# A gated mix of softmax attention and a gated linear unit on Trainium2: row maxima closed per 512 queries and 16 steps ahead, block products added one period later, token sums loaded in quarters, 16 zero products at the start

## The chip, the cores and the metric

The kernel runs on one core of one Trainium2 chip. The metric is the device time of one execution in microseconds, less being better. Before the change three runs took 1696.09, 1696.15 and 1697.68 us; their median is 1696.15 us.

## What is computed

```python
x = A_x                                              # (1, 2048, 512), fp32
g = sigmoid((x * gate_w).sum(-1, keepdims=True))
qkv = x @ wqkv                                       # 32 heads of 16
p = softmax(q @ k.T * 16 ** -0.5)                    # per head, 2048 x 2048
a = (p @ v) @ wo
h = sigmoid(x @ w_gate) * (x @ w_up)                 # 1792 wide
b = h @ w_down
return g * a + (1 - g) * b
```

All of it is fp32. The kernel splits each operand of a large product into a rounded part (h) and its remainder (l) and adds three products: h with h, h with l, l with h.

## The kernel before

**Stages.** The work has four stages, one after the other on TensorE.

1. *Start.* WARM products of zeros (L82) run while the first inputs load; then come the q and k projections of the first 8 heads (L134) and the values of two token tiles.
2. *Head.* The values of the other 14 token tiles are made two tiles at a time. Each pair of tiles takes two groups of 12 pairs of 64-row products (L147), one group for each half of the rows (LOW, UP). Into these groups calls of `first_max` are put. One call makes two products of scores with 48 rows each (L277), one for each head of the pair or for two tiles of the second head, and VectorE takes the maximum of each over 512 keys (L279, `stat`).
3. *Periods.* 256 periods follow. Two heads make a pair of heads, there are 16 pairs, and each pair takes 16 periods. A period makes eight tiles of scores, transposed, with 64 rows, of which two hold the negative row maxima (L670); ScalarE takes their exponentials (L672); 32 narrow products multiply them with the values (L687, `values`). It also makes eight score products and their maxima (L277, L279) for periods still to come, so that a maximum is ready when the exponent needs it. The gaps of TensorE are filled with the rest of the dense work, piece by piece (`filling`): first 24 projections of two periods each (`Sum`, L147), then 196 block products of one period each (`Side`, L167). These block products form the gate and up products by a scheme with seven instead of eight block products, on sums of token blocks (`xm`) and sums of weight blocks (`mh`, `ml`).
4. *Final.* The down projection, and the heads' outputs (L880).

**What sets the order.** Each engine runs its instructions in the order in which the program writes them. Within a period the order on TensorE is written out as words in STEADY: m0 and m1 are a score product with its maximum (`mx`), t0 and t1 a transposed score tile with its exponential (`st_part`), d0 and d1 a half row of the dense work, `turn` a token on GpSimd. The word `work` and a call at the end of each period pop entries from the list `later`: GpSimd operations that belong to the dense work (splits of weights, sums of blocks, sums of tokens). The last TAIL periods have the order LAST, which has no m words. The bank of PSUM that a product takes follows from a fixed recurrence (`given`, REUSE).

**The maxima.** `sm_step` numbers 512 steps. A step is one tile of 128 queries against 1024 keys for both heads of a pair: two calls. In the head of the program the first FIRST steps of pair 0 are made for both heads, those to UPPER for the second head only; from then on `mx(0)` and `mx(1)` go on from there, four products each a period. So the maxima lead the scores by FIRST steps, two steps a period, and the last FIRST/2 periods have no maxima left to make; these are the TAIL periods. When all maxima of one head over 1024 queries are there (32 of them, `full`), `turn_max` (L288 to L301) ends them: VectorE takes the maximum over the four key blocks (L291) and transposes it (L293), GpSimd splits it into two parts (L98, L99), and SyncE stores it (L296, `m_d`) and loads it back as two rows of `qs` (L300). `turn_max` runs after the end of a period.

**Dense helpers.** `mixing` makes sums of token blocks: it loads pieces of x, adds them on GpSimd and stores them in `xm_d`; `mixed` (L350 to L353) loads such a sum of 2 MB as one DMA. `combine` adds block products: its `arrive` puts additions on GpSimd (L399) as soon as the eviction of the product has been written (L494, ScalarE). `split_later` (L121, L124) splits weights on GpSimd, a cast to the rounded part and a subtraction.

Of the kernel before, what the change touches and what calls it, by code (L numbers as in the profile page):

```python
# [35 lines left out]
FIRST = 20  # L36
WARM = 20
# [9 lines left out]
def gated_mix(ctx, tc, x, xc, wqk, wv, wo, w_gu, w_down, gate_w, out):  # L47
# [28 lines left out]
    m_d = dram.tile([NPAIR, 2, 2, P, 2, 32], F32, name="m_d")  # L76
# [187 lines left out]
    def sm_step(j):  # L264
# [5 lines left out]
        def one(b, i):  # L270
            half = (p, qt // 8, b)
            if half not in stat:
                stat[half] = keep.tile([P, 8, 4], F32, name=f"stat{p}_{qt // 8}_{b}", tag="stat", bufs=4)
                count[half] = 0
            r, g = 64 * b, 2 * kh + i
            t = bankm()
            pe.matmul(t, qs[r:r + KM, qt * P:(qt + 1) * P], ks[r:r + KM, g * 512:(g + 1) * 512],  # L277
                      start=True, stop=True)
            dve.tensor_reduce(stat[half][:, qt % 8, g:g + 1], t, axis=AX.X, op=ALU.max)  # L279
            count[half] += 1  # L280
            if count[half] == 32:
                full.append(half)
# [4 lines left out]
    def turn_max():  # L287
        half = full.pop(0)  # L288
        p, i, b = half
        m = square()  # L290
        dve.tensor_reduce(m[:, :8], stat.pop(half), axis=AX.X, op=ALU.max)  # L291
# [6 lines left out]
        for a in range(2):  # L298
            r = 64 * b + 3 * DH + a
            sp.dma_start(QS[p % 2][r:r + 1, i * 1024:(i + 1) * 1024].bitcast(F32).rearrange(  # L300
                "o (t g j) -> o t g j", g=4, j=32), rows[a, :8].unsqueeze(0))  # L301
# [7 lines left out]
    def mixing(pair):  # L309

        def piece(j, b):
# [9 lines left out]
            def add(rows, op):  # L321
                pool.tensor_tensor(f[rows, 0, :], f[rows, 0, :], f[rows, 1, :], op)

            def low():
                pool.tensor_tensor(e[:, 0, :], f[:, 0, :], f[:, 1, :], ALU.subtract)
                sp.dma_start(xm_d[pair, j, :, :, b, :], f)
            ops = []
            signs = [MIX[j][1 - g][1] for g in (LOW, UP)]
            if signs[0] == signs[1]:
                rows = [slice(0, P)]  # L330
            else:
                rows = SIDES
            for r, sign in zip(rows, signs):
                if sign:
                    ops.append(lambda r=r, op=ALU.add if sign == "+" else ALU.subtract: add(r, op))
            ops.append(lambda: pool.tensor_copy(e[:, 1, :], f[:, 0, :]))
            ops.append(low)
            return ops

        ops = []  # L340
        for j in range(4):
            for b in range(4):
                nxt = piece(j, b)
                later.extend(ops)
                ops = nxt
                yield
        later.extend(ops)
        yield

    def mixed(pair, j):  # L350
        t = xp.tile([P, 2, KT, 512], F32R, name=f"xm{pair}_{j}", tag="xt", bufs=4)
        sp.dma_start(t.bitcast(F32), xm_d[pair, j])
        return t  # L353

# [69 lines left out]
    def filling():  # L424
# [41 lines left out]
        t = 0  # L466
        for cp in range(2):
            for fp in range(NF // 2):
                for a in range(2):
# [3 lines left out]
                    for q, (j, g) in enumerate(order):  # L473
# [7 lines left out]
                        arrive(m, e)  # L481
# [5 lines left out]
                        if cp == 0 and fp == NF // 2 - 1 and a == 1 and q in (2, 4, 6):  # L487
                            late_t[q // 2 - 1] = mixed(1, q // 2 - 1)
                if cp == 0 and fp == NF // 2 - 1:
                    late_t[3] = mixed(1, 3)  # L490
                    T = late_t
        wd.extend(split_weights(raw_weights(w_down[f * P:(f + 1) * P, :], [P, D], f"wd{f}")) for f in range(2))
# [439 lines left out]
```

## Time and profile before

| what | time in us |
|---|---|
| median of three runs | 1696.15 |
| the profiled execution | 1695.68 |
| its span, first to last instruction | 1693.4 |
| start: zero products, then real ones from 8.33 | 0.92 to 35.65 |
| head: values of 14 tiles with 44 calls of `first_max` | 35.65 to 91.02 |
| passage from the head to the first `values` | 91.02 to 97.95 |
| periods: 256 `values`, the last one starts at | 1491.68 |
| final stage to the end of the span | 1493.6 to 1693.4 |

The profile is that of one execution. Its own time is 0.47 us below the median of the runs, and 2.3 us of it lie outside the span. Engines are named PE (TensorE), DVE (VectorE), ACT (ScalarE), POOL (GpSimd) and SP (SyncE, which only issues DMAs here). Over the whole span PE has work in hand for 99%, DVE for 84%, ACT for 79%, POOL for 59%. Products of PE overlap, so a busy PE can still be one that waits for a bank of PSUM; the start times of its products tell more than the busy share.

### The profile page before, as it was taken

To read this page: it belongs to the slowest core of one execution; us is meant where nothing else is said; L and a number is where in the kernel's file an instruction comes from. 1 tells how busy PE (TensorE), PEld (TensorE's weight loads), DVE (VectorE), ACT (ScalarE), POOL (GpSimd) and SP (SyncE) were. 2 spreads that over 40 slices of the span, in tenths; PEclk is the share of its full clock that TensorE was granted. 3 is DMA by queue.
4 is the path that set the end of the run, shared out by engine and by line. 5 is a ranking of instruction groups with operands and counts; after the bars stand their busy time and mean duration, and the time that the engine had idled before them with its cause. 6 is when DMAs were issued, how large, how long until landed. Compare 5 with 4: busy or idle time off the path is not lost.

```text
span 1693.4 us, 42705 instructions
## 1 busy us (share of the span) xinstructions
PE 1683.5 (99%) x16556; PEld 1151.9 (68%) x16556; DVE 1427.4 (84%) x2321; ACT 1338.7 (79%) x2677; POOL 999.7 (59%) x1065
## 2 busy tenths in 40 slices
PE   9999999999999999999999999999999999999998
PEld 8766666666666666666666666666666666478887
DVE  5988898898898898898898899888889889757543
ACT  4178888888888888888888899999999989974321
POOL 1036665357878787766666667777776665442110
PEclk9999999999999999999999999999999999999999
DMA  9514776363545454442447242524242522367752
GB/s 259 111 51 156 177 246 192 109 186 103 131 136 129 142 142 132 118 125 78 98 136 239 71 122 83 113 83 110 87 112 84 116 89 97 97 220 240 243 192 67
DMA packets 132170, 229.55 MB, mean 136 GB/s; under 512 B 30784, under 2 KB 47424, under 8 KB 127936
## 3 DMA queue, kind: packets, MB, share of 16 engines
q1 hardware_dynamic: 131680, 226.30, 46.8%
q8 instruction: 130, 2.13, 0.5%
q14 instruction: 72, 0.59, 0.1%
q10 hardware_dynamic: 288, 0.52, 0.1%
HBM read 148.90 MB, written 77.86 MB: 134 GB/s over the span
## 4 chain that ended last, share of the span: by engine, by line
PE 96%; DVE 3%; ACT 1%; issue 0%; POOL 0%; DVEq 0%; POOLq 0%; ACTq 0%
PE dn L167 23%; PE sm L687 22%; PE sm L277 9%; PE st L277 8%; PE st L687 7%; PE sm L880 7%; PE dn L147 6%; PE sm L670 4%; PE st L134 4%; PE st L670 3%; DVE stat L279 3%; PE dn L880 2%; ACT p L672 1%; PE st L147 0%; PE st L82 0%
## 5 line engine op out<-in xcount | busy, mean ns | idle before, releaser
L279 DVE TENSOR_REDUCE stat<-sm 128x1 f32<-128x512 f32 x1129 | 726.6, 682 | 68.7 <-PE sm L277 26.7
L672 ACT ACTIVATE p<-sm 128x512 f32<-128x512 f32 x1211 | 675.6, 638 | 2.2 <-PE sm L670 0.3
L279 DVE TENSOR_REDUCE stat<-st 128x1 f32<-128x512 f32 x919 | 600.3, 683 | 71.2 <-PE st L670 28.3
L672 ACT ACTIVATE p<-st 128x512 f32<-128x512 f32 x837 | 494.2, 643 | 10.5 <-PE st L670 9.4
L167 PE MATMUL dn<-xm,mh 64*128 64x512 f32 x1568 | 485.3, 389 | 0.0
L670 PE MATMUL sm<-qs,ks 64*128 64x512 f32 x1211 | 436.3, 404 | 0.3 <-ACT p L672 0.2
L277 PE MATMUL sm<-ks,qs 48*128 48x512 f32 x1129 | 412.4, 421 | 1.2 <-DVE stat L279 0.7
L687 PE MATMUL sm<-p,v 128*17 128x256 f32 x6176 | 370.9, 380 | 0.1
L277 PE MATMUL st<-ks,qs 48*128 48x512 f32 x919 | 352.1, 426 | 0.7 <-ACT p L672 0.7
L670 PE MATMUL st<-qs,ks 64*128 64x512 f32 x837 | 318.9, 409 | 1.5 <-ACT v L539 1.4
L167 PEld LDWEIGHTS dn<-xm,mh 64*128 64x128 f32 x1568 | 289.6, 185 | 29.2
L167 PE MATMUL dn<-xm,ml 64*128 64x512 f32 x784 | 304.0, 388 | 0.0
L687 PEld LDWEIGHTS sm<-p,v 128*17 128x17 f32 x6176 | 162.8, 97 | 172.2 <-ACT p L672 59.4
L277 PEld LDWEIGHTS sm<-ks,qs 48*128 48x128 f32 x1129 | 201.2, 184 | 91.4 <-DVE stat L279 78.6
L399 POOL TENSOR_TENSOR m<-m,m 128x512 f32<-128x512 f32 x140 | 178.2, 1290 | 92.5 <-ACT m L494 66.6
L670 PEld LDWEIGHTS sm<-qs,ks 64*128 64x128 f32 x1211 | 217.6, 185 | 18.8 <-ACT p L672 3.7
L277 PEld LDWEIGHTS st<-ks,qs 48*128 48x128 f32 x919 | 164.7, 185 | 83.9 <-DVE stat L279 66.9
L670 PEld LDWEIGHTS st<-qs,ks 64*128 64x128 f32 x837 | 152.6, 185 | 15.8 <-ACT v L539 1.9
L699 POOL TENSOR_TENSOR sum<-sum,part 128x256 f32<-128x256 f32 x192 | 141.2, 736 | 26.9 <-ACT part L695 18.5
L98 POOL CAST mhl<-mt 128x32 fp32r<-128x32 f32 x64 | 13.4, 210 | 235.7 <-DVE mt L293 158.4
L167 PEld LDWEIGHTS dn<-xm,ml 64*128 64x128 f32 x784 | 144.4, 184 | 11.8
L121 POOL TENSOR_TENSOR ml<-r,mh 128x512 fp32r<-128x512 f32 x112 | 143.8, 1284 | 7.4
(220 smaller groups left out, 2275.1 us busy)
## 6 DMA issues: line engine op xcount, KB each, us to landing
r<-in_w_gu_dram SPq DMA_DIRECT2D x280, 128.0 KB
gul<-gu_d SPq DMA_DIRECT2D x56, 512.0 KB
gu_d<-m SPq DMA_DIRECT2D x84, 256.0 KB
xm_d<-xm SPq DMA_DIRECT2D x32, 512.0 KB
xm<-xm_d SPq DMA_DIRECT2D x8, 2048.0 KB
xm<-in_xc_dram SPq DMA_DIRECT2D x104, 128.0 KB
qs<-q_d SPq DMA_DIRECT2D x90, 128.0 KB
ks<-k_d SPq DMA_DIRECT2D x90, 128.0 KB
```

The costliest lines, as they stand in the source:

```text
L121: pool.tensor_tensor(l, src, h.bitcast(F32), ALU.subtract)
L134: pe.matmul(o, a, b, start=(i == 0), stop=(i == len(ops) - 1))
L147: mm = pe.matmul(self.o, a[rows], b[rows], start=(self.n == 0), stop=(self.n == 2 * len(self.ops) - 1))
L167: pe.matmul(self.o, a, b, start=(self.n == 0), stop=(self.n == len(self.ops) - 1))
L277: pe.matmul(t, qs[r:r + KM, qt * P:(qt + 1) * P], ks[r:r + KM, g * 512:(g + 1) * 512], start=True, stop=True)
L279: dve.tensor_reduce(stat[half][:, qt % 8, g:g + 1], t, axis=AX.X, op=ALU.max)
L399: pool.tensor_tensor(o, x, y, op)
L670: pe.matmul(o, ks[r:r + KR, (kt + a) * P:(kt + a + 1) * P], qs[r:r + KR, c * 512:(c + 1) * 512], start=True, stop=True)
L672: act.activation(pt[:, a, :], o, AF.Exp, scale=DH ** -0.5)
L687: pe.matmul(o[r:r + VW, :], v[:, 4 * k % 16 + a, h * VW:(h + 1) * VW], pts[b][:, a, 256 * i:256 * i + 256], start=(a == 0), stop=(a == 3))
L699: pool.tensor_tensor(s, s, e, ALU.add)
L880: pe.matmul(down[t], a, b, start=(f == 0 and m == 0), stop=(f == NF - 2 and m == 5))
```

## The change

Six edits:

- WARM goes from 20 to 16.
- FIRST goes from 20 to 16, and with it UPPER from 24 to 20, TAIL from 10 to 8, the word order LAST to one for all tail periods (without d words), and EARLY, the period from which parts of the final stage are prepared, from 242 to 244. The calls of `first_max` fall from 44 to 36. They stand at the start and at m = 5 of each group, and from t = 8 also at m = 8; before at the start, at 5 and at 11, and from t = 12 also at 8.
- `turn_max` ends the maxima of one head over 512 queries instead of 1024: 128 turns instead of 64, each with 4 columns instead of 8, and rows of `qs` half as long.
- `arrive` is called one block product later.
- The loads of `mixing` become entries of `later`, one entry for each piece, instead of being issued at once when the piece before is queued.
- A sum of tokens is loaded in four quarters, which pass through a list `parts` and from there, one or two for each dense product, into `later`; before, it was one DMA that was issued at once.

The diff, cut to its core:

```diff
-FIRST = 20
-WARM = 20
+FIRST = 16
+WARM = 16
 TAIL = FIRST // 2
...
-            half = (p, qt // 8, b)
+            part = (p, qt // 4, b)
...
-            if count[half] == 32:
-                full.append(half)
+            if count[part] == 16:
+                full.append(part)
...
-        dve.tensor_reduce(m[:, :8], stat.pop(half), axis=AX.X, op=ALU.max)
+        dve.tensor_reduce(m[:, :4], stat.pop(part), axis=AX.X, op=ALU.max)
...
-        ops = []
-        for j in range(4):
-            for b in range(4):
-                nxt = piece(j, b)
-                later.extend(ops)
-                ops = nxt
-                yield
-        later.extend(ops)
+        pieces = [(j, b) for j in range(4) for b in range(4)]
+        loaded = []
+        later.append(lambda: loaded.append(load(*pieces[0])))
+        for n, (j, b) in enumerate(pieces):
+            yield
...
+            later.append(lambda n=n, j=j, b=b: low(loaded[n], j, b))
+            if n + 1 < len(pieces):
+                later.append(lambda n=n: loaded.append(load(*pieces[n + 1])))
         yield
 
     def mixed(pair, j):
         t = xp.tile([P, 2, KT, 512], F32R, name=f"xm{pair}_{j}", tag="xt", bufs=4)
-        sp.dma_start(t.bitcast(F32), xm_d[pair, j])
+        for b in range(4):
+            parts.append(lambda b=b: sp.dma_start(t[:, :, b, :].bitcast(F32), xm_d[pair, j, :, :, b, :]))
         return t
+
+    parts = []
+
+    def take(n):
+        while parts and n:
+            later.append(parts.pop(0))
+            n -= 1
...
-                    if runs in (14, 16, 23):
+                    if runs in (14, 17, 22, 24):
                         T[len(T)] = mixed(0, len(T))
-        T[3] = mixed(0, 3)
+                    take(2 if runs > 21 else 1)
...
-                        arrive(m, e)
+                        if arrived:
+                            arrived.pop(0)()
+                        arrived.append(lambda arrive=arrive, m=m, e=e: arrive(m, e))
...
+                        take(2)
...
-    first = [(j, i) for j in [*range(0, 16, 2), *range(1, 16, 2), *range(16, FIRST), *range(FIRST, UPPER, 2)] for i in range(2)]
+    first = [(j, i) for j in [*range(0, FIRST, 2), *range(1, FIRST, 2), *range(FIRST, UPPER, 2)] for i in range(2)]
...
-                if m in (5, 11) or t >= 12 and m == 8:
+                if m == 5 or t >= 8 and m == 8:
                     first_max()
...
-    LAST = ["t0 d1 t0 d1 t0 d1 d1 turn work t0 t1 t1 d0 t1 d0 t1 d0 d0"] * (TAIL - 4) + [
+    LAST = ["t0 t0 t0 work t0 t1 t1 t1 t1"] * TAIL
```

Two places show how instructions move. The first is on PE, in the head, at the end of the first group (t = 2, LOW) and the start of the next. The L147 rows are the token values, the L277 rows the score products of the calls. Before:

```order
L147 MATMUL st_67<-wv_l,xt_138 128x512
L147 MATMUL dn<-wv_l,xt_138 128x512
L147 MATMUL st_67<-wv_h,xt_138 128x512
L147 MATMUL dn<-wv_h,xt_138 128x512
L277 MATMUL sm_69<-ks_108,qs_107 128x512
L277 MATMUL sm_70<-ks_108,qs_107 128x512
L277 MATMUL sm_71<-ks_108,qs_107 128x512
L277 MATMUL sm_72<-ks_108,qs_107 128x512
```

And now, at the same place:

```order
L147 MATMUL st_67<-wv_l,xt_134 128x512
L147 MATMUL dn<-wv_l,xt_134 128x512
L147 MATMUL st_67<-wv_h,xt_134 128x512
L147 MATMUL dn<-wv_h,xt_134 128x512
L277 MATMUL sm_69<-ks_104,qs_103 128x512
L277 MATMUL sm_70<-ks_104,qs_103 128x512
L147 MATMUL st_67<-wv_h,xt_134 128x512
L147 MATMUL dn<-wv_h,xt_134 128x512
```

Two calls in a row, the last of one group and the first of the next, have become one.

The second place is on POOL, in the periods of the projections, where the k weights of column block 2 (`k2h`, `k2l`) are split for their second projections. The names `xm` and `qk` are token sums and evicted projections, `sum` is the running sum of `values`, and `mhl` is the split of maxima in `turn_max`. Before:

```order
L336 CAST xm_3_1_3120<-xm_3_1_3120 128x512
L325 TENSOR_TENSOR xm_3_1_3120<-xm_3_1_3120 128x512
L124 CAST k2h<-k2r 128x512
L121 TENSOR_TENSOR k2l<-k2r,k2h 128x512
L699 TENSOR_TENSOR sum_3_3220<-sum_3_3220,part_3377 128x256
L232 CAST qh_3_3428<-qk_1_1_1_3426 128x512
```

And now (L340, L328 and L708 are L336, L325 and L699 before):

```order
L340 CAST xm_3_1_3397<-xm_3_1_3397 128x512
L328 TENSOR_TENSOR xm_3_1_3397<-xm_3_1_3397 128x512
L124 CAST k2h<-k2r 128x512
L98 CAST mhl_2_1_3638<-mt_2_1_3636 128x32
L99 TENSOR_TENSOR mhl_2_1_3638<-mt_2_1_3636,mhl_2_1_3638 128x32
L121 TENSOR_TENSOR k2l<-k2r,k2h 128x512
L708 TENSOR_TENSOR sum_0_3586<-sum_0_3586,part_3670 128x256
L232 CAST qh_3_3478<-qk_1_1_1_3476 128x512
```

The subtraction that makes `k2l` now stands behind a turn of maxima, the one that follows the end of period 33; the projection that uses `k2l` begins with period 34. Before, the pair was popped in period 30.

More of the change, by code (lines that the diff above doesn't have):

```diff
@@ L270, in one @@
         def one(b, i):
-            half = (p, qt // 8, b)
-            if half not in stat:
-                stat[half] = keep.tile([P, 8, 4], F32, name=f"stat{p}_{qt // 8}_{b}", tag="stat", bufs=4)
-                count[half] = 0
+            part = (p, qt // 4, b)
+            if part not in stat:
+                stat[part] = keep.tile([P, 4, 4], F32, name=f"stat{p}_{qt // 4}_{b}", tag="stat", bufs=8)
+                count[part] = 0
             r, g = 64 * b, 2 * kh + i
@@ L278, in one @@
                       start=True, stop=True)
-            dve.tensor_reduce(stat[half][:, qt % 8, g:g + 1], t, axis=AX.X, op=ALU.max)
-            count[half] += 1
-            if count[half] == 32:
-                full.append(half)
+            dve.tensor_reduce(stat[part][:, qt % 4, g:g + 1], t, axis=AX.X, op=ALU.max)
+            count[part] += 1
+            if count[part] == 16:
+                full.append(part)
         return one
@@ L287, in turn_max @@
     def turn_max():
-        half = full.pop(0)
-        p, i, b = half
+        part = full.pop(0)
+        p, i, b = part
         m = square()
-        dve.tensor_reduce(m[:, :8], stat.pop(half), axis=AX.X, op=ALU.max)
+        dve.tensor_reduce(m[:, :4], stat.pop(part), axis=AX.X, op=ALU.max)
         mt = keep.tile([P, 32], F32, name=f"mt{p}_{i}_{b}", tag="mt", bufs=2)
@@ L745, in gated_mix @@
     given = [seven[sorted(set(given[-20:])).index(b)] for b in given[-20:]]
-    LAST = ["t0 d1 t0 d1 t0 d1 d1 turn work t0 t1 t1 d0 t1 d0 t1 d0 d0"] * (TAIL - 4) + [
-        "t0 d1 t0 d1 t0 d1 turn work t0 t1 t1 d0 t1 d0 t1 d0"] * 4
-    parts = {"m0": mx(0), "m1": mx(1), "d0": dense(LOW), "d1": dense(UP)}
+    LAST = ["t0 t0 t0 work t0 t1 t1 t1 t1"] * TAIL
+    group = {"m0": mx(0), "m1": mx(1), "d0": dense(LOW), "d1": dense(UP)}
     bank = turns(banks)
```

44 lines of the change are left out of this document (21 added, 23 removed).

## The prediction

> **What bounds the kernel now.** I read the page first, then the busy time in windows that each lie within one stage, then the timelines of the engines at the places that the change touches. The page's busy times and the chain that ended last:
>
> ```profile
> PE 1683.5 (99%) x16556; PEld 1151.9 (68%) x16556; DVE 1427.4 (84%) x2321; ACT 1338.7 (79%) x2677; POOL 999.7 (59%) x1065
> PE 96%; DVE 3%; ACT 1%; issue 0%; POOL 0%; DVEq 0%; POOLq 0%; ACTq 0%
> ```
>
> The chain is PE nearly throughout, but this is an average. The 3% of DVE has a place. Columns of the windows: busy us and count of PE, PEld, DVE, ACT, POOL, then clock, DMA share and GB/s.
>
> ```profile
> 40.00:60.00 20.00, 19.91 (x167) 15.90 (x165) 19.97 (x34) 3.26 (x6) 0.00 (x0) 1.00 0.79 158
> 100.00:1440.00 1340.00, 1340.00 (x14572) 888.89 (x14574) 1205.54 (x2064) 1186.46 (x2440) 923.35 (x1004) 1.00 0.45 126
> 1450.00:1490.00 40.00, 39.85 (x396) 19.70 (x390) 24.20 (x22) 39.35 (x86) 13.83 (x15) 1.00 0.31 99
> ```
>
> In the head DVE is busy for 19.97 of 20 us. In the periods no engine but PE is full (DVE 1205.54, ACT 1186.46 of 1340 us). In the tail periods it is ACT, 39.35 of 40. So a maximum taken out of the head is worth DVE's time for it, in a period it is worth nothing by itself, and the price of a period differs between steady and tail. Starts of `values` on PE, two in the steady part, two where dense work and the maxima of the second head have run out, two in the tail:
>
> ```profile
> 699.62 1.92 PE L687 MATMUL sm<-p,v 128*17 128x256 f32 x32
> 705.13 1.92 PE L687 MATMUL sm<-p,v 128*17 128x256 f32 x32
> ...
> 1444.36 1.92 PE L687 MATMUL sm<-p,v 128*17 128x256 f32 x32
> 1449.88 1.92 PE L687 MATMUL sm<-p,v 128*17 128x256 f32 x32
> ...
> 1482.92 1.92 PE L687 MATMUL sm<-p,v 128*17 128x256 f32 x32
> 1487.12 1.92 PE L687 MATMUL sm<-p,v 128*17 128x256 f32 x32
> ```
>
> A steady period takes 5.51 us, one without dense work 5.52 as well, a tail period 4.20.
>
> **Zero products (20 to 16).** The zero products alone, in windows (PE and PEld), and PE's timeline around them:
>
> ```profile
> 3.90:6.90 3.00, 3.00 (x8) 2.37 (x8) 1.00 1.05 399
> 6.90:8.30 1.40, 1.40 (x7) 1.02 (x6) 1.00 1.04 386
> ```
> ```profile
> 0.92 7.58 PE L82 MATMUL st<-warm 128*128 128x512 f32 x20 [0.92 <-DVE warm L79]
> 8.33 0.62 PE L134 MATMUL st<-xt,q0h 128*128 128x512 f32 x2
> ...
> 35.65 0.50 PE L277 MATMUL sm<-ks,qs 48*128 48x512 f32 x2
> ```
>
> Until 6.9 they come some 0.43 us apart (8 touch 3.0 us), behind that 0.22 (7 touch 1.4). The last four are fast ones: 4 x 0.22 = 0.87 us, and the first real product moves from 8.33 to about 7.46. Its inputs are there: the first remainder of x starts on DVE at 5.41 and two of them take 1.29.
>
> ```profile
> 5.41 1.29 DVE L99 TENSOR_TENSOR xt<-x,xt 128x512 fp32r<-128x512 f32 x2
> ```
>
> I take -0.87; the bounds are 0 (an input comes last) and -1.7 (four at the slow spacing). The Trainium skill (TensorE: Matmul & The Clock Gate, Part 1) says that the warm-up is about 3.4 us of time in a free-running window, not a number of products, and that its length varies between runs. This trace has about 6 us of it, so the page's figure isn't met here; what it would change is a rival below.
>
> **The head (44 calls to 36).** DVE's timeline:
>
> ```profile
> 39.41 36.59 DVE L279 TENSOR_REDUCE stat<-sm 128x1 f32<-128x512 f32 x60 [0.33 <-PE sm L277]
> 75.92 0.18 DVE L291 TENSOR_REDUCE msq<-stat 128x8 f32<-128x32 f32 x1
> ...
> 76.58 14.40 DVE L279 TENSOR_REDUCE stat<-sm 128x1 f32<-128x512 f32 x24
> ```
>
> 84 reduces run without a gap, 0.61 and 0.60 us each, so a call costs 1.21; the two turns between them cost 76.58 - 75.92 = 0.66. PE without a wait shows only at the start:
>
> ```profile
> 35.98 0.40 PE L147 MATMUL st<-wv_h,xt 64*128 64x512 f32 x1
> ...
> 37.37 0.40 PE L277 MATMUL sm<-ks,qs 48*128 48x512 f32 x2
> ...
> 38.98 0.65 PE L277 MATMUL sm<-ks,qs 48*128 48x512 f32 x4
> ```
>
> Six pairs of L147 take 37.37 - 35.98 = 1.39, a call with six pairs 38.98 - 37.37 = 1.61, the call alone 0.22 to 0.23. A group with two calls is then 2 x 1.61 = 3.22 us on PE, against 2 x 1.21 = 2.42 on DVE: PE sets it. With three calls it is 3.45 against 3 x 1.21 = 3.63: DVE sets it. After the change there are six groups with two calls, 6 x 3.22 = 19.3, and eight with three. DVE's part of these is 24 x 1.21 = 29.0 plus four turns, 4 x 0.33 = 1.3. The last call now has three pairs of L147 behind it instead of six (before, the last group's list was already empty at m = 8), so PE leaves about 0.23 x 3 = 0.7 us earlier against DVE: 48.9 in all, and 0.3 until DVE's first maximum of the second part. Before it was 91.02 - 35.65 = 55.4. I take -6.1, with -4.5 (eight groups at 6 x 0.61 = 3.66 and no 0.7 at the end, and the passage gives back 1) and -6.9 (of the turns only a third falls on the chain) as bounds. What comes next is late by nothing new: the passage waits for ACT, which has two evictions to do, and DVE's copy at its end has over 2 us until PE needs the bank.
>
> ```profile
> 91.02 0.61 PE L670 MATMUL st<-qs,ks 64*128 64x512 f32 x2
> 93.07 0.73 PE L670 MATMUL st<-qs,ks 64*128 64x512 f32 x2 [1.44 <-ACT v L539]
> ```
>
> **Two tail periods become steady ones.** The 16 steps missing from the head's lead return as two periods at the end with m words: 2 x (5.52 - 4.20) = +2.64. They have no dense work, but neither has 1444.36 to 1449.88. Bounds +1.5 and +2.64.
>
> **The hiccup at a change of heads.** In period 32 PE waited at a score product for the row of maxima, whose load was issued at 268.31:
>
> ```profile
> 268.31 1.47 SPq L300 DMA_DIRECT2D qs<-m_d  x2
> ```
> ```profile
> 268.98 1.92 PE L687 MATMUL st<-p,v 128*17 128x256 f32 x32
> 274.79 1.92 PE L687 MATMUL sm<-p,v 128*17 128x256 f32 x32
> ```
>
> 5.81 instead of 5.51. With 512 queries a row is closed four periods ahead for the first head, where two were left: -0.30. Bounds 0 and -0.30.
>
> **128 turns instead of 64.** Each adds an L291, an L293, two small POOL operations and three small DMAs on SP. A period with a turn beside the place where a period has none:
>
> ```profile
> 701.39 0.18 DVE L291 TENSOR_REDUCE msq<-stat 128x8 f32<-128x32 f32 x1
> ...
> 702.00 1.29 DVE L279 TENSOR_REDUCE stat<-st 128x1 f32<-128x512 f32 x2
> ...
> 707.52 0.69 DVE L279 TENSOR_REDUCE stat<-sm 128x1 f32<-128x512 f32 x1 [0.64 <-PE st L670]
> ```
>
> The first reduce after the turn starts 2.38 us behind its `values` (702.00 - 699.62), without a turn 2.39 (707.52 - 705.13). DVE's 0.64 idle hides it: 0. Without that cover each costs about 0.33 as in the head, 64 x 0.33 = 21 us.
>
> **Additions one product later.** Where an addition now stands at the head of POOL's queue until ACT has written the eviction, that wait goes. POOL has 923.35 of 1340 us of work in the periods, so this is 0 by itself. Each buffer of `er` lives a period longer; with six of them the eviction has periods to spare.
>
> **Loads as entries of `later`, in quarters.** Every load now takes a slot, the list is longer, and splits of weights come later than before. For most this is hidden by two periods or more. One is not: `k2l` of period 34 is behind the turn that follows period 33. How such a place runs is seen one turn earlier, where a period starts on PE at 204.64 and uses its first remainder at 205.45:
>
> ```profile
> 204.64 0.49 PE L277 MATMUL sm<-ks,qs 48*128 48x512 f32 x1
> ...
> 205.45 0.39 PE L147 MATMUL dn<-xt,q3l 64*128 64x512 f32 x1
> ```
> ```profile
> 205.30 0.26 POOL L99 TENSOR_TENSOR mhl<-mt,mhl 128x32 fp32r<-128x32 f32 x1
> 205.50 0.61 POOL L232 CAST qh<-qk 128x512 fp32r<-128x512 f32 x1
> ...
> 213.22 1.28 POOL L121 TENSOR_TENSOR q1l<-q1r,q1h 128x512 fp32r<-128x512 f32 x1
> ```
>
> After the turn POOL is free at 205.50; the split takes 1.28, so `k2l` would be ready at 206.8, 1.35 behind 205.45. Behind the waiting product stand all score products of the period, and ACT and DVE wait for them. I take +1.4; bounds 0 and +2. The quarters must land before their period. The last quarters of the second set stand behind loads of maxima rows in SP's queue, which wait for their stores, and these for POOL. By the order a few us are left for each: 0, with rival D for the case that they aren't.
>
> **The final stage.** Its preparation on ACT, DVE and POOL starts two tail periods later against the end, 2 x 4.20 = 8.4 us. From 1450 to 1490 DVE has 24.20 of 40 us of work and POOL 13.83, so both catch up: 0, bounds 0 and +2.
>
> **Sum.** -0.87 - 6.1 - 0.30 + 2.64 + 1.4 = -3.2 us on the profiled 1695.68: 1692.5. The median of the runs is 0.47 above the profiled execution, so 1692.9 for a median. A measurement of this kernel can tell about 0.2% from no change, that is 3.4 us, or below 1692.8: the forecast lies on this bound.
>
> **The rivals.**
>
> *A. The stall in period 34 is hidden or small.* For it: POOL's times are rough, and the product can be late by what the banks leave. Against it: in period 32 a late product cost nearly all of its delay. -4.6, 1691.5. Chance 0.25.
>
> *B. The zero products end differently.* If slow spacing lasted 3.4 us, 8 products would be slow and 8 fast, 3.4 + 1.8 us, and the first real one could start at 6.1, 1.3 earlier than I count: -4.5, 1691.6. It is the rule of the Trainium skill's page above; the trace speaks against it with 6 us. Chance 0.05.
>
> *C. The head gains less.* The new turns and the copies at its end sit on PE's path, and the head saves only 4.5: -1.6, 1694.5. The chain's 3% of DVE and the 84 reduces without a gap speak against it. Chance 0.21.
>
> *D. Quarters and weights arrive late: slower.* If the last quarter of a sum is issued more than about 4 us into the period before its use, PE waits at the first products of each of the four tiles of the second set, and at some of the weight sums, which by the order are now two periods ahead where they were more. With 2 us for each of four tiles that is +8 - 3.2 = +4.8: 1701. It decides when waits reach 6.6 us in sum. For it: SP's queue is the one that gets longer, with waits for POOL ahead of loads. Against it: the DMA engines were 45% busy over the periods. Chance 0.12.
>
> *E. The turns cost on DVE after all,* 21 us: 1714. DVE's 90% in the periods speak for it, the rows at 702.00 against it. Chance 0.03.
>
> **Chances.** My own forecast has 0.34 and lies on the bound: half of it counts as faster, half as no change. With A and B that makes 0.17 + 0.25 + 0.05 = 0.47 faster; with C 0.17 + 0.21 = 0.38 no change; D and E are 0.15 slower. The likeliest is 1692.9. The range takes in A, B and C with their bounds and half of D, and leaves out E and the farther half of D, and A and B together at the other end: 1690.4 to 1698.0.
>
> **What would show it.** The first real product at 7.5; L277's first row at 34.8 and the first L670 near 84.0; the first `values` near 91.0; period 32 at 5.51; period 34 at 6.9 with PE waiting for `k2l`; eight tail periods of 4.20. Wrong would be: turns that move the reduce after them, waits of PE for `xm` near period 146 to 153, or a steady period other than 5.51.

## The result and the profile after

The changed kernel is slower: a median of 1710.44 us (1708.96 to 1712.35, 6 runs) against 1696.12 us before (1695.67 to 1697.68, 6 runs), a ratio of 1.0084 with a 95% interval of 1.0071 to 1.0097. The profiled execution took 1710.80 us with a span of 1709.0. The forecast was 1692.9, in a range that ended at 1698.0.

In the profile's chain of work that ended last, DMA and POOL now have shares, where they had none or 0%:

```profile
PE 92%; DVE 3%; DMA 2%; POOL 1%; ACT 1%; SPq 0%; issue 0%; POOLq 0%; DVEq 0%; ACTq 0%
```

The start and the head. First PE's timeline of the zero products, then DVE's in the head (the rows at 54.48 and 56.13 are the last with a gap ahead of them):

```profile
0.92 5.81 PE L82 MATMUL st<-warm 128*128 128x512 f32 x16 [0.92 <-DVE warm L79]
6.57 0.64 PE L134 MATMUL st<-xt,q0h 128*128 128x512 f32 x2
```
```profile
34.55 1.29 DVE L279 TENSOR_REDUCE stat<-sm 128x1 f32<-128x512 f32 x2 [4.54 <-PE sm L277]
...
54.48 1.29 DVE L279 TENSOR_REDUCE stat<-sm 128x1 f32<-128x512 f32 x2 [0.35 <-PE sm L277]
56.13 13.28 DVE L279 TENSOR_REDUCE stat<-sm 128x1 f32<-128x512 f32 x22 [0.36 <-PE sm L277]
...
80.25 4.99 DVE L279 TENSOR_REDUCE stat<-sm 128x1 f32<-128x512 f32 x8
```

The first real product starts at 6.57, 1.76 us earlier: 0.87 by four products less, the rest because the slow stretch of the zero products is shorter in this execution. DVE has gaps until 56.13, so PE sets the pace in the groups with two calls; from there DVE runs through.

The passage from the head to the periods, in windows of PE (columns: busy us and count, granted clock, DMA share, GB/s):

```profile
84.00:88.00 4.00, 2.30 (x11) 0.88 0.28 67
88.00:92.00 4.00, 4.00 (x20) 0.50 0.00 0
92.00:96.00 4.00, 4.00 (x46) 0.76 0.02 4
```

Here stands something that the profile of before did not have, a granted clock of 0.50. The first score product of the periods is at 84.65, the first `values` at 94.10: 9.45 us, where it was 6.94.

Period 33 to 34. The starts of `values` on PE and PE's wait in between, then POOL:

```profile
276.20 1.92 PE L696 MATMUL st<-p,v 128*17 128x256 f32 x32
...
280.22 0.50 PE L147 MATMUL dn<-xt,k2l 64*128 64x512 f32 x1 [0.95 <-POOL k2l L121]
...
283.11 1.92 PE L696 MATMUL sm<-p,v 128*17 128x256 f32 x32
```
```profile
278.69 0.26 POOL L99 TENSOR_TENSOR mhl<-mt,mhl 128x32 fp32r<-128x32 f32 x1
278.90 1.27 POOL L121 TENSOR_TENSOR k2l<-k2r,k2h 128x512 fp32r<-128x512 f32 x1
```

6.91 us, PE waiting for `k2l` behind the turn: this is what was forecast, to 0.01 us.

The largest loss is at the change to the second set of token sums, periods 147 to 152. PE's starts of `values` and its two longest waits, and SP's queue at the same time:

```profile
906.80 1.92 PE L696 MATMUL sm<-p,v 128*17 128x256 f32 x32
911.77 0.49 PE L167 MATMUL dn<-xm,mh 64*128 64x512 f32 x1 [1.14 <-DMA xm<-xm_d]
916.14 0.50 PE L167 MATMUL dn<-xm,mh 64*128 64x512 f32 x1 [3.40 <-DMA xm<-xm_d]
917.86 2.91 PE L696 MATMUL sm<-p,v 128*17 128x256 f32 x32
...
953.87 1.92 PE L696 MATMUL st<-p,v 128*17 128x256 f32 x32
```
```profile
900.41 1.24 SPq L349 DMA_DIRECT2D xm<-xm_d  x2
901.75 0.54 SPq L296 DMA_DIRECT2D m_d<-mhl  x1
...
904.37 0.56 SPq L349 DMA_DIRECT2D xm<-xm_d  x1
909.88 1.36 SPq L300 DMA_DIRECT2D qs<-m_d  x2
911.29 0.58 SPq L349 DMA_DIRECT2D xm<-xm_d  x1
```

Six steady periods are 33.10 us; from 906.80 to 953.87 there are 47.07. So 13.97 us are lost here. The third quarter of a sum is issued at 904.37, the fourth at 911.29: between them SP stands at the load of a maxima row until the store of 901.75 has landed.

Not all of the 13.97 us are waits. PE is idle for 8.7 us of them, in five waits for `xm`. Behind the waits the granted clock falls to 0.50 twice, for 10.2 us in all; the row at 917.86 shows it, where 32 narrow products take 2.91 us instead of 1.92. The clock (third number from the end) in the two places:

```profile
916.00:920.00 4.00, 3.86 (x32) 0.57 0.89 263
944.00:950.00 6.00, 5.64 (x42) 0.50 0.42 143
```

At half clock pairs of products start 0.43 us apart (from 88.47 to 88.90, for example) where it is 0.23 at full clock, so PE gets through about half of its work, and these 10.2 us cost up to 5.1 (an estimate). With the 8.7 that makes 13.8, nearly the whole loss.

The tail. Starts of `values`, and the clock in between:

```profile
1472.52 3.32 PE L696 MATMUL st<-p,v 128*17 128x256 f32 x32
1477.73 1.92 PE L696 MATMUL sm<-p,v 128*17 128x256 f32 x32
1481.93 1.92 PE L696 MATMUL sm<-p,v 128*17 128x256 f32 x32
```
```profile
1474.00:1476.00 2.00, 2.00 (x22) 0.50 0.09 19
```

The first tail period takes 5.21 us at half clock (its `values` alone 3.32 instead of 1.92); before it took 3.67. Of the profiled executions of the runs below, five have 3.4 us of half clock in their tail as well (e1_defer, e1_quarters, e2_fill, e2_first, e3_arrive); the others have none there.

All differences of the two profiled executions, in us, from first products and from starts of `values`:

| part | forecast | measured |
|---|---|---|
| start, to the first L277 (35.65 to 34.01) | -0.87 | -1.6 |
| head (55.37 to 50.64) | -6.1 | -4.7 |
| passage (6.94 to 9.45) | 0 | +2.5 |
| period 32 (5.82 to 5.52) | -0.30 | -0.3 |
| period 33 to 34 (5.52 to 6.91) | +1.4 | +1.4 |
| periods 147 to 152 | 0 | +14.0 |
| `values` of period 245 to 255 (41.81 to 45.97) | +2.64 | +4.2 |
| one period of 5.70, and after the last `values` | 0 | 0 |
| sum | -3.2 | +15.5 |

The profiled times differ by 15.1 us.

### The profile page after: what moved, and what is told of

Its sections match the earlier page's. It is cut to its first block, busy times and chain, and to the rows that moved or that the text cites. A ratio compares the mean times of both kernels' runs of the same rounds, so it can differ in the third digit from the quotient of the medians.

```text
span 1709.0 us, 43428 instructions
## 1 busy us (share of the span) xinstructions
PE 1691.1 (99%) x16552; PEld 1157.5 (68%) x16552; DVE 1449.4 (85%) x2449; ACT 1339.8 (78%) x2677; POOL 1023.5 (60%) x1193
## 4 chain that ended last, share of the span: by engine, by line
PE 92%; DVE 3%; DMA 2%; POOL 1%; ACT 1%; SPq 0%; issue 0%; POOLq 0%; DVEq 0%; ACTq 0%
PE dn L167 22%; PE sm L696 21%; PE sm L277 9%; PE st L277 8%; PE st L696 7%; PE dn L147 6%; PE sm L888 5%; PE sm L679 4%; PE st L134 4%; PE st L679 3%; DVE stat L279 2%; PE dn L888 2%; PE st L147 1%; DMA m_d<-mhl 1%; DMA xm<-xm_d 1%; DMA late<-in_w_down_dram 0%
## 5 line engine op out<-in xcount | busy, mean ns | idle before, releaser
L279 DVE TENSOR_REDUCE stat<-st 128x1 f32<-128x512 f32 x929 | 606.8, 683 | 71.1 <-PE st L277 32.5
L681 ACT ACTIVATE p<-st 128x512 f32<-128x512 f32 x834 | 492.5, 639 | 15.1 <-PE st L679 10.5
L277 PE MATMUL sm<-ks,qs 48*128 48x512 f32 x1119 | 407.5, 421 | 0.0
L277 PE MATMUL st<-ks,qs 48*128 48x512 f32 x929 | 358.0, 428 | 0.5 <-ACT p L681 0.5
L98 POOL CAST mhl<-mt 128x32 fp32r<-128x32 f32 x128 | 26.8, 209 | 425.8 <-DVE mt L293 345.0
L277 PEld LDWEIGHTS sm<-ks,qs 48*128 48x128 f32 x1119 | 198.1, 185 | 84.3 <-DVE stat L279 60.0
L277 PEld LDWEIGHTS st<-ks,qs 48*128 48x128 f32 x929 | 167.4, 186 | 83.9 <-DVE stat L279 65.9
L708 POOL TENSOR_TENSOR sum<-sum,part 128x256 f32<-128x256 f32 x192 | 141.1, 735 | 24.2 <-ACT part L704 17.8
```

What stands on the lines that cost most here:

```text
L279: dve.tensor_reduce(stat[part][:, qt % 4, g:g + 1], t, axis=AX.X, op=ALU.max)
L681: act.activation(pt[:, a, :], o, AF.Exp, scale=DH ** -0.5)
L708: pool.tensor_tensor(s, s, e, ALU.add)
```

## The experiments

Three theories stood for the 14 us. *List*: the quarters come late because they pass through `parts` and `later`. *SP*: SP's queue is held, by loads of maxima rows that wait for their store and by the number of DMAs. *Bandwidth*: four quarters land more slowly than one DMA. For the passage the *clock* theory: the two gaps of PE in it let the clock fall to half. (The expectations below put these gaps at 2.5 us; in the traces they are 1.7 to 1.9, of which the longest is 1.44.) "Excess" below is the time from `values` of period 147 to that of period 153 less 33.10 us, in the profiled execution, so it holds for that one execution; the times are medians. Medians of before are from the same chip, 1695.5 to 1695.7.

**Quarters at once** (e1_direct):

```diff
             parts.append(lambda b=b: sp.dma_start(t[:, :, b, :].bitcast(F32), xm_d[pair, j, :, :, b, :]))
+        while pair and parts:
+            parts.pop(0)()
         return t
```

> The changed kernel, with the quarters of the second set of token sums issued at once instead of through `parts` and `later`. In the changed kernel the periods 147 to 152 take 14 us more than six steady ones, PE waiting for xm<-xm_d. List theory (the quarters come late because they pass through the list): that excess falls under 2 us, time about 1697 to 1699. SP theory (loads of maxima rows hold SP's queue until their store has landed, whatever is queued behind): the excess stays above 6 us, time 1702 or more. Bandwidth theory (four quarters are slower to land than one DMA of 2 MB): excess unchanged, 1710.

1705.94 us (1702.31 to 1707.95), ratio 1.0054 [1.0037, 1.0070]; excess 9.94 (`values` at 907.13 and 950.17). The list theory falls as the whole cause: 4 us go, 10 stay.

**Maxima rows loaded a period later** (e1_defer):

```diff
+        held.append(lambda: back(p, i, b, rows))
+        if not holding:
+            held.pop(0)()
+    def back(p, i, b, rows):
         for a in range(2):
...
+        holding.append(k)
+        while held:
+            held.pop(0)()
         while full:
             turn_max()
```

> The changed kernel, with the loads of maxima rows (qs<-m_d) issued a period later than their store, when the store has landed, so that SP does not stand at them. SP theory: the excess of periods 147 to 152 falls from 14 us to 4 or less, time about 1700. List theory: the excess stays above 10 us, time 1707 to 1710. Either way the periods 33 to 34 keep their 1.4 us and the clock of 0.5 near 90 us stays.

1698.79 us (1695.56 to 1704.45), ratio 1.0022 [1.0011, 1.0034]; excess 3.23. Most of the loss goes when SP does not stand at the rows; that is what the SP theory expected. The wide spread says that the excess is not the same in each execution. The clock in the passage is still half.

**Turns per 512 queries alone, in the kernel before** (e1_turns): `stat` by four tiles, `full` at 16, half rows, as in the diff of the change.

> The kernel before, with turns per 512 queries alone (128 instead of 64). If a turn costs only what DVE can hide: 1696 plus or minus 1, with the 0.3 us of period 32 gone. If turns hold SP's queue enough by themselves: PE waits for xm or mh appear and the time is 1699 or more. If each turn costs its DVE time: 1714.

1699.39 us (1696.52 to 1702.42), ratio 1.0016 [1.0006, 1.0025]. Excess 0.01, no PE wait for xm, all but a few periods at 5.52. Of the profiled execution's 1.8 us (1697.45) the passage takes 1.4 (8.30), the head 0.8 with two turns more, one period 1.1 (6.59); the 0.3 of period 32 is gone, and the stretch behind the last `values` is 1.2 shorter (200.6). So 64 more turns cost the steady periods nothing, but for the one of 6.59, in which PE waits 0.94 us for a DMA. SP stands longer at the rows (10.8 us from 868 to 945, before 1.6). The median is 3.7 us above that of before and its interval leaves out no change; the profiled execution shows about half of this, and where the other half lies stays open.

**Quarters through the list alone, in the kernel before** (e1_quarters): `mixed` and `take` as in the change, 64 turns.

> The kernel before, with the token sums loaded in quarters through `parts` and `later` alone (64 turns, loads of pieces at once). List theory: the waits for xm<-xm_d near period 146 to 153 appear here too, 5 us or more, time 1701 or more. SP theory: half the turns leave SP free, waits under 3 us, time 1696 to 1699.

1701.16 us (1699.74 to 1704.96), ratio 1.0027 [1.0014, 1.0039]; 4.8 us are lost between `values` of period 143 and 153 of the profiled execution, which at 1704.96 is the slowest of the six. Of these 1.9 are one wait of PE for `xm`, and up to 1.7 go with 3.4 us at half clock. Neither expectation came true as it stands; but quarters cost without any new turn, about a third of what they cost with them.

**Both cures together** (e2_both): rows a period later, and quarters at once.

> The changed kernel with both: loads of maxima rows a period later than their store, and the second set of token sums issued at once. The first alone left an excess of 3.2 us in periods 147 to 152 (profiled 1699.0), the second alone 9.9 us (1704.5). If SP's queue is all of it: excess under 1 us, profiled time 1695 to 1697. If landing itself is short of bandwidth: 2 to 3 us stay, 1698 to 1699.

1700.45 us (1698.81 to 1701.79), ratio 1.0024 [1.0015, 1.0033]; excess 4.73. The two don't add up. In this execution most of the loss lies in period 147 (9.62 us). PE's one wait there is for a maxima row:

```profile
910.86 0.47 PE L688 MATMUL sm<-qs,ks 64*128 64x512 f32 x1 [2.31 <-DMA qs<-m_d]
```

The row's load, put off by a period, now comes late in SP's queue itself, and 3.4 us at half clock follow.

**Pieces' loads at once, beside rows a period later** (e2_loads): `mixing` as before the change.

> The changed kernel with loads of maxima rows a period later, and with the loads of pieces of x issued at once as before the change, not as entries of the list. Prediction's theory (the list is longer, so the split of k2 falls behind the turn): period 33 to 34 goes from 6.91 back to 5.52, time 1.4 us under the same kernel without this edit (profiled 1699.0, median 1698.8), so about 1697.5. Rival (the turn itself delays POOL there): it stays at 6.9.

1697.42 us (1695.17 to 1700.20), ratio 1.0009 [1.0000, 1.0018]. The starts of `values` of periods 33 and 34:

```profile
276.43 1.92 PE L707 MATMUL st<-p,v 128*17 128x256 f32 x32
281.94 1.92 PE L707 MATMUL sm<-p,v 128*17 128x256 f32 x32
```

5.51 us, where e1_defer has 6.93: the stall of `k2l` comes from the loads' entries in the list, as forecast. Excess 3.58.

**The head and tail alone** (e2_first): the kernel before with turns per 512, FIRST = 16, and the new `first`, calls and LAST; WARM 20, additions, pieces and token sums as before.

> The kernel before with turns per 512 queries, FIRST of 16, the new places of the calls in the head and the new order of the tail; WARM, loads, additions and the load of token sums are as before. Against the kernel with the turns alone (profiled 1697.45, median 1699.4): head 4.5 to 5 us shorter, tail 2.6 longer, so 2 us less: 1695.5 profiled, if the clock in the passage is the same. Rival (the head's gain is lost in the passage or the tail): no change or slower, 1697 to 1700.

1692.81 us (1692.16 to 1694.43), ratio 0.9981 [0.9971, 0.9990], faster than before by 2.9 us in the median. Against e1_turns 2 us were expected; the medians differ by 6.6 and the profiled executions by 4.6, of which 1.4 are the passage, at full clock here; the rest stays open. Head 50.71, passage 6.93 at full clock, tail part 45.90, excess 0.00.

**Zero products in the passage** (e2_fill), beside rows a period later:

```diff
     next(ahead)
     next(ahead)
+    for _ in range(7):
+        pe.matmul(maxb[0], z.to_broadcast([P, P]), z.to_broadcast([P, 512]), start=True, stop=True)
...
     for _ in ahead:
         pass
+    for _ in range(3):
+        pe.matmul(maxb[0], z.to_broadcast([P, P]), z.to_broadcast([P, 512]), start=True, stop=True)
```

> The changed kernel with loads of maxima rows a period later, and with ten more zero products in the passage from the head to the periods, where PE waits for ACT. Clock theory (PE idle for 2.5 us in the passage lets the clock fall to half for 6.8 us): the granted clock stays 1.0 there, the passage takes 7.0 us instead of 8.3 to 9.5, and runs of one kernel differ less; time 1 to 2.5 us under the same kernel without them (median 1698.8). Rival (the passage is long because PE waits for DVE or rows of maxima): the passage stays at 8.3 or more, or grows by the zero products.

1699.43 us (1696.68 to 1702.20), ratio 1.0019 [1.0010, 1.0028]. The same windows of PE as above, with the zero products:

```profile
84.00:88.00 4.00, 4.00 (x21) 1.00 0.23 68
88.00:92.00 4.00, 4.00 (x30) 1.00 0.00 0
92.00:96.00 4.00, 4.00 (x50) 1.00 0.01 4
```

PE is busy throughout, the clock stays at 1.00, and the passage takes 7.45 us instead of 8.30. That is what the clock theory expected, and of the 14 profiled executions without zero products there 12 fell to half clock. The median did not fall, against the expectation (1699.43 for 1698.79). In the profiled execution the excess is 7.67 against 3.23, which is far more than the 0.85 us; but at 1702.18 this execution is one of the two slowest of its ten, so for the others that isn't shown.

**One DMA for each token sum, at once** (e3_whole): the only edit to the changed kernel.

```diff
-        for b in range(4):
-            parts.append(lambda b=b: sp.dma_start(t[:, :, b, :].bitcast(F32), xm_d[pair, j, :, :, b, :]))
+        parts.append(lambda: sp.dma_start(t.bitcast(F32), xm_d[pair, j]))
+        while pair and parts:
+            parts.pop(0)()
```

> The changed kernel with each token sum loaded by one DMA of 2 MB, those of the second set at once; loads of pieces stay entries of the list, loads of maxima rows stay right behind their store. The four quarters at once left an excess of 9.9 us in periods 147 to 152. If the quarters as such are to blame (more entries in SP's queue and in the DMA queue ahead of a maxima row's store): excess under 1 us, time about 1696. If the pieces' loads and turns alone fill the queue: excess above 5 us, time 1702 or more.

1695.20 us (1693.69 to 1697.27), ratio 0.9996 [0.9987, 1.0005]. `values` of periods 147 and 153:

```profile
907.08 1.27 PE L697 MATMUL sm<-p,v 128*17 128x256 f32 x20
...
940.17 1.92 PE L697 MATMUL st<-p,v 128*17 128x256 f32 x32
```

33.09 us, no excess. 1710.44 to 1695.20, 15.2 us, with the turns and all else as changed. Two things are undone here, the quarters and, for the second set, the way through the list. Against e1_direct, which issues at once as well, it is the quarters alone: excess 9.94 to 0. e4_list below keeps the list.

**16 zero products alone, in the kernel before** (e3_warm): WARM = 16.

> The kernel before with 16 zero products instead of 20, nothing else. Prediction's term: 0.87 us less, 1694.9 against 1695.7. Clock theory: the first real product moves by 0.9 to 1.8 us and the time by no more than that, but where the clock's window falls differently in the passage, the passage is 1.4 to 2.6 us longer in some runs: 1694 to 1697, runs of one kernel differing by over 2 us.

1695.79 us (1693.89 to 1697.68), ratio 0.9999 [0.9990, 1.0008]: no change. In the profiled execution the first real product starts at 6.16, 2.2 us earlier, and the first L277 1.3 us earlier; the passage takes 8.32 us, 1.4 more than in the profile of before. The passage has this length with 20 zero products too (e1_turns, e1_quarters, e3_arrive), so it is not their doing. And the interval, from 1.7 us faster to 1.4 slower, can't tell the expected 0.87 from nothing.

```profile
88.00:92.00 4.00, 2.57 (x17) 1.00 0.25 66
92.00:96.00 4.00, 3.54 (x17) 0.63 0.00 0
```

**Additions one product later, in the kernel before** (e3_arrive).

> The kernel before with additions of block products one product later, nothing else. Prediction's term: 0, 1695.7 within 0.7 us. Rival (buffers of er are held a period longer and evictions wait): 1697 or more, with ACT waiting for POOL at L494.

1695.05 us (1694.04 to 1696.31), ratio 0.9995 [0.9986, 1.0004]: no change, as forecast.

**The version that the runs point to** (e3_best): e2_first with additions one product later, 16 zero products at the start, and seven (five and two) in the passage.

> The version that the runs point to: the kernel before with turns per 512 queries, FIRST of 16 with its places in the head and tail, additions one product later, 16 zero products at the start and seven in the passage; token sums and pieces are loaded as before the change. Clock theory: median about 0.9 us under the same without the last three (1692.8), 1691.5 to 1692.5, and less spread; if the zero products in the passage only cost their own time: 1693 or more.

1691.72 us (1690.70 to 1692.92, 11 runs), ratio 0.9973 [0.9964, 0.9982]: faster than both kernels, by 4.0 us against before. The passage takes 7.02 us. The spread, 2.2 us, is about that of e2_first (2.3); that part of the expectation did not come true. Which of the three edits brings the 1.1 us against e2_first was not tried apart.

**One DMA, through the list** (e4_list): `parts.append` of one whole load, no loop at once.

> The changed kernel with each token sum loaded by one DMA of 2 MB that passes through `parts` and `later` like the quarters did. Immediate quarters left an excess of 9.9 us in periods 147 to 152, an immediate whole load none. If passing through the list costs by itself: excess 4 us or more, time 1699 or more. If only the quarters cost: excess under 1 us, about 1695.2.

1696.42 us (1692.07 to 1698.01), ratio 1.0003 [0.9994, 1.0012]; excess 2.14. Neither expectation quite. Against e3_whole it is 1.2 us more in the median and 2.14 in the excess, so the list may cost 1 to 2 us by itself, though the intervals overlap; 11.8 of the 13.97 us go with the quarters alone.

**Four DMAs with long pieces** (e4_rows):

```diff
-            parts.append(lambda b=b: sp.dma_start(t[:, :, b, :].bitcast(F32), xm_d[pair, j, :, :, b, :]))
+            parts.append(lambda r=r: sp.dma_start(t[r].bitcast(F32), xm_d[pair, j, r]))
+        while pair and parts:
+            parts.pop(0)()
```

> The changed kernel with the second set in four DMAs at once again, but each of 32 partitions by 16 KB in a row instead of 128 partitions by two pieces of 2 KB. If the small pieces are what makes quarters slow (148944 packets instead of 132170 in the whole execution): excess of periods 147 to 152 under 2 us, time 1695 to 1697. If it is the number of DMAs in SP's queue: excess stays near 9.9 us, time 1703 to 1706.

1709.86 us (1709.15 to 1710.24), ratio 1.0080 [1.0063, 1.0097]; excess 14.09. The packets of the execution are nearly as few as with whole loads (141776 against 141391), and the loss is as large as in the changed kernel. So small pieces are not needed for it. But this run does not single out the number of DMAs: its long pieces move less while the DMA engines are full. Here, with whole loads, and with the quarters of small pieces at once (e1_direct), each in 10 us full of sums (the last two numbers are DMA share and GB/s):

```profile
920.00:930.00 10.00, 5.34 (x49) 0.85 1.01 211
```
```profile
910.00:920.00 10.00, 10.00 (x116) 1.00 1.00 391
```
```profile
920.00:930.00 10.00, 7.87 (x81) 0.87 0.98 324
```

So these quarters also land more slowly, and part of the 14.09 may be due to that; the excess was expected near 9.9. What the number of DMAs does is seen in what SP waits for. SP's waits from 868 to 930 us in this kernel (us in total, times, longest), and with whole loads:

```profile
SPq L241 <- DMA xm<-xm_d: 6.9, 4, 2.5
...
SPq L300 <- DMA m_d<-mhl: 4.3, 2, 2.8
SPq L408 <- DMA xm<-xm_d: 4.0, 2, 2.0
SPq L372 <- DMA xm<-xm_d: 2.9, 2, 1.8
```
```profile
SPq L300 <- DMA m_d<-mhl: 13.8, 4, 8.1
...
SPq L370 <- DMA xm<-xm_d: 4.1, 1, 4.1
```

L241 loads rows of q and k for the next pair of heads, L408 stores block sums, L372 loads weights: none of them reads xm, and yet they wait until a quarter has landed, eight times for 13.8 us, where the whole loads hold three other DMAs for 5.9 (4.1, 1.1 at a store and 0.7 at a row). The kept traces show why. SP's DMAs use eight semaphores in turn, and one that comes to a semaphore waits until the DMA eight places ahead of it has landed; in each run all but four of its 1250 to 1466 DMAs keep to this turn, and all eight waits are of this kind. So in these programs SP has at most eight DMAs under way, and a quarter takes as much of that room as a whole load does. It reaches PE by the held stores: ACT can't evict until one has landed, and PE waits for ACT:

```profile
939.18 0.60 ACT L506 ACTIVATE m<-dn 128x512 f32<-128x512 f32 x1 [6.57 <-DMA gu_d<-m]
```
```profile
939.83 0.79 PE L167 MATMUL dn<-xm,mh 64*128 64x512 f32 x1 [5.44 <-ACT m L506]
```

In the changed kernel it is the rows at which SP stands; loads and stores held behind an unrelated quarter make only 0.5 us there. From 868 to 945 us in it and, for comparison, before:

```profile
SPq L300 <- DMA m_d<-mhl: 23.4, 5, 5.6
```
```profile
SPq L300 <- DMA m_d<-mhl: 1.6, 1, 1.6
```

With whole loads SP stands 13.8 us at the rows too, and PE loses nothing. The rows alone don't make the loss, nor does the list; together with four times as many DMAs behind them they do.

The excess in its two parts, PE's idle time and its time at half clock, in us:

| run | excess | PE idle | at half clock |
|---|---|---|---|
| the changed kernel | 13.97 | 8.7 | 10.2 |
| e4_rows | 14.09 | 10.1 | 10.2 |
| e1_direct | 9.94 | 5.5 | 6.8 |
| e2_fill | 7.67 | 4.3 | 6.8 |
| e2_both | 4.73 | 2.4 | 3.4 |
| e2_loads | 3.58 | 3.4 | 0 |
| e1_defer | 3.23 | 3.1 | 0 |
| e4_list | 2.14 | 1.3 | 0 |

Idle time and half of the time at half clock add up to the excess within 1.2 us. The bandwidth theory by itself does not hold: e1_defer has the quarters of the changed kernel, and 10.7 of the 13.97 us are gone in its profile.

## Why the prediction was wrong

**The quarters** are the step that failed: "By the order a few us are left for each: 0". 14.0 us were measured. The place and the queue were right, and the rival D for it, with the order of SP's queue read correctly. But the "few us" were set against no landing time at all. The only store whose row the working looked at is that of period 32 in the kernel before, in a quieter stretch; its row is loaded 2.2 us later (266.11 to 268.31):

```profile
266.11 0.54 SPq L296 DMA_DIRECT2D m_d<-mhl  x1
```

At the change of token sums twelve loads of rows for the next pair of heads, the weights and the sums are under way together, and a store of maxima takes 8.1 us (901.75 to 909.88) until its row can be loaded. With that the last quarters come late, PE waits 8.7 us for them, and the half clock behind the waits adds up to 5.1, which no term and no rival had. That a DMA holds up others that have nothing to do with it was no part of the working either. The price for D, 2 us for each of four tiles, was 8, close to the 8.7 of waits, but 14.0 were lost; its chance of 0.12 was low, and the range ended below its 1701.

**The passage** was taken as moving along unchanged, at full clock. It is not a constant: 6.9 us at full clock (before, e2_first), 8.3 (six kernels) with 3.4 us of half clock, or 9.5 (six kernels) with 6.8. The rows of before that I quoted, 91.02 and 93.07 with PE idle for 1.44 us, show the gap; what it can do to the clock they did not show, since the profiled execution of before was spared. The Trainium skill (TensorE: Matmul & The Clock Gate, Part 1) says that the clock is set by how busy PE was in a free-running window of about 3.4 us. The half clock after the passage, from 87.1 to 93.9 by finer windows, is two such windows long, that of the kernels with 8.3 is one, and its hitting or missing the same gap agrees with a window that is not tied to the program. The prediction used this rule of the Trainium skill for the start alone. In the profiles compared, half clock costs 2.5 us in the passage, 1.6 in the tail and up to 5.1 at the token sums: up to 9.2 of the 18.7 us between the forecast sum of -3.2 and the measured +15.5.

**Zero products.** The term -0.87 was about right, but one profiled row was not enough to say so. The first real product starts between 6.2 and 7.5 us in the eleven profiled executions with 16, and between 6.9 and 8.3 in the five with 20; the first L277 comes at 34.4 and 35.2 on average, 0.8 us earlier. The -1.6 of the two profiles compared is that and luck. Whether the whole kernel gains it the medians can't tell (e3_warm, ratio 0.9999, with an interval from 1.7 us faster to 1.4 slower).

**The head** was right in its mechanism and short by 1.4 us in size: -4.7 for -6.1, near the bound of -4.5. The six groups with two calls take 54.48 - 34.55 = 19.9 us for 19.3; DVE fills up one call later than I assumed (0.4); and the 0.5 us from the first product to the first maximum, which are in the old 55.37, were missing in the new sum.

**Period 33 to 34, period 32 and the additions** came as forecast: +1.39, -0.30, no change by the additions. The turns cost the steady periods nothing in the profiles, as forecast; but with the turns alone the median rose by 3.7 us (e1_turns), half of it unexplained. e2_loads shows that the stall of `k2l` is due to the loads' entries.

**The tail** came as forecast where the clock stayed up: the ten periods from 245 took 44.33 us in e3_whole, +2.5 for +2.64. In the changed kernel's profile the first tail period fell into a stretch at half clock, +1.6. In before it did not.

Without the quarters, and with the second set issued at once, the changed kernel takes 1695.20: 2.3 us above the forecast, inside its range, and no clear change, between -0.13% and +0.05%; with the pieces' loads, the additions and the zero products undone as well, and the passage spared in the profile, the 1692.81 of e2_first.

The excess differs between executions of kernels that treat the token sums alike (3.23, 3.58 and 7.67 with rows a period later) mainly by the half clock: the waits in them are 3.1, 3.4 and 4.3 us, and only the last has 6.8 us at half clock. What stays open: what decides whether a wait brings the half clock, the second half of e1_turns' 3.7 us, and how much of e4_rows' loss is slow landing. A load of the quarters from another queue was not tried.

## What to carry to other kernels

Split a load only if its queue has room: here SP has eight DMAs under way at most, four quarters of a sum take four of these places where a whole load takes one, and quarters stand behind rows that wait for their store; the change lost 14 us by it, for nothing gained. Reckon a queue with the landing times of its busiest stretch, and write the figure down: "a few us are left" is no comparison without it. A stretch of 2 us or so in which PE is mostly idle should be priced with the half clock that may follow it, even if the one execution at hand was spared; filling the one in the passage with products of zeros cost 0.1 to 0.5 us here, and the half clock costs 1.4 to 2.6 where it hits.

## What the runs showed of the hardware

Two gaps of PE in the passage, 1.9 us together and at the same place of the program, were followed by half clock in 12 of the 14 profiled executions in which they were not filled, for 3.4 us in six and 6.8 in six; in the two with the gap filled the clock stayed at 1.00. Waits at the token sums were followed by half clock as well, of 10.2 us in the changed kernel; but 2.4 us of waits in e2_both brought 3.4 us of it and 3.4 us of waits in e2_loads brought none. The zero products at the start, 16 of the same kind from 0.92 us on, ended so that the first real product began anywhere between 6.16 and 7.53 us in eleven kernels. And a store of maxima rows, issued at 901.75 in a stretch with a DMA share of 0.96 (900 to 910), held the load behind it until 909.88, where in period 32 of the kernel before a row was loaded back 2.2 us after its store was issued.
